# Two Mlps behind a delta-rule attention: three PSUM banks each for h and for the sums, an earlier third copy, and two steps moved from VectorE to GpSimd

## The chip, the core and the metric

The kernel runs on one core of a Trainium2 chip. The metric is the time of one execution in microseconds (us), here the median of three runs. A core has five engines with queues of their own, each strictly in order: TensorE (PE: matmuls, and PEld for the loads of their weights), VectorE (DVE), ScalarE (ACT), GpSimd (POOL) and SyncE (SP, which issues the DMAs). PE multiplies from SBUF into PSUM, which has eight banks of 128 partitions x 512 fp32 values. The engines wait for each other through semaphores.

## The reference

Three parts in a row, all in fp32; only the second is touched by the change, and it is the one shown in full.

```
attn: delta rule over 768 steps for 4 x 8 heads of 48 -> x [3072, 384]

def _moe_ref(x, w_in, w_out, a, b):          # first Mlp, d_ff = 2048
    h = x @ w_in
    P = a[0] + a[1]*h + a[2]*h**2 + a[3]*h**3
    Q = 1.0 + abs(b[0])*abs(h) + abs(b[1])*h**2
    g = P / (Q + 1e-6)
    return g @ w_out

def _moe2_ref(x, w_in, w_out):               # second Mlp
    h = x @ w_in
    return (h * tanh(softplus(h))) @ w_out
```

The weights come as 64-bit floats and are turned into two fp32 parts on the chip.

## The kernel before

**Splitting.** PE multiplies in a reduced fp32 format. So each operand is kept as a high part (a cast) and a low half (what the cast lost, a subtraction), and each product is three matmuls: high x high, high x low, low x high.

**Units.** The 3072 tokens are 6 groups of 512, and d_ff is 16 blocks of 128. A unit is one group and one block: 96 units per Mlp, numbered in the order of work, 16 to a group. For a unit PE forms h in one bank (9 matmuls, line 893) and, four units later, adds g times the second weights to three sums of the group (9 matmuls, line 1002). A sum takes a bank for 16 units. After the last unit of a group ACT copies the three sums out (line 1124, `ev`), and SP stores them.

**A unit of the first Mlp on the other engines.** ACT: magnitude of h (line 924, `q`), r = b1 q + b0 (line 931, or on POOL, line 927), s = a3 h + a2 (line 933). POOL: q = q r (line 937). ACT: Ln (line 945) and Exp with a minus sign (line 947), which give 1/Q. DVE: five steps for P and for g (lines 952, 954, 961, 965, 970); line 954 is the last to read h, so it frees h's bank. ACT casts g to its high part (line 904), POOL forms g's low half (line 908). r is on POOL in odd units, and also in the even unit of the three in which x is prepared.

**What sets the order.** Two strings, MLP_OPS, give the order in which the operations of one iteration are issued, and LAGS tells by how many units each lags behind: "u" is h, "d" the sums, "y" the copies, 1a 1b 1c magnitude, r and s, 1d q, 1e 1f Ln and Exp, 1g to 1k DVE's steps, 1L and 1m the parts of g. Each engine gets its own operations in that order and keeps to it. Within ACT, Ln and Exp of a unit stand ahead of the magnitude of the next.

**Around it.** "xa" and "xB" prepare the next group's x (line 873 casts on ACT, line 877 forms the low half); "fx" loads it. "c" and "f" convert the second Mlp's weights, half of them (16 sides) during the first: a side is a magnitude on ACT (line 739), clamp and shift on DVE (lines 744, 748), two more steps on DVE (754, 760), a cast on ACT (767) and a remainder on POOL (772, `wt`). `calm` lists the iterations in which a side goes on. In PSUM, `Ring` hands out 2 banks for h, 4 for sums and 2 for r in turn: `ps.add(ps2, h=2, o=4, r=2)`. With four banks for three sums, the first sum of a group starts in a bank that nobody holds.

Of the kernel before, what the change touches and what calls it, by code (L numbers as in the profile page):

```python
# [9 lines left out]
F32 = mybir.dt.float32  # L10
# [22 lines left out]


MLP_OPS = [
    "fx fw y0 y1 1e 1f u0 u1 u2 1a 1b 1c 1i 1j 1k 1d 1g 1h y2 d0 d1 d2 d3 xa 1L 1m xB f c",
    "fx fw y0 1e 1f y1 2a 2b u0 u1 u2 1i 1j 1k y2 d0 v0 2M d1 v1 d2 v2 d3 v3 xa 1L 1m xB f c",
]
LAGS = {
# [6 lines left out]
class Ring:  # L46
# [6 lines left out]
    def add(self, pool, **bufs):  # L53
        for tag, b in bufs.items():
            slots = self.slots.setdefault(tag, [])
            self.n[tag] = len(slots)
            slots.extend((pool, b) for _ in range(b))

    def tile(self, shape, dtype, tag):
        i = self.n[tag]  # L60
        self.n[tag] = (i + 1) % len(self.slots[tag])
        pool, b = self.slots[tag][i]
        return pool.tile(shape, dtype, tag=tag, name=tag, bufs=b)


# [628 lines left out]
class Weights:  # L694
# [5 lines left out]
    LEAST = 2.0 ** -15  # L700
    MOST = 1.875 * 2.0 ** 16
    free = False
    word = None

    def __init__(self, nc, w_in, w_out, sb, kept, passing, scratch):
# [14 lines left out]
    def convert(self, f, side):  # L720
        nc = self.nc
        w = {}

        def get():
            w["raw"] = self.sb.tile([128, 3, 128], I64, "w64")
            src = self.w_out[f * 128:(f + 1) * 128] if side else self.w_in[:, :, f * 128:(f + 1) * 128]
            nc.sync.dma_start(out=w["raw"], in_=src)

        def word(i):
            return w["raw"].rearrange("p k c -> p (k c)").bitcast(I32).rearrange("p (n t) -> p n t", t=2)[:, :, i]  # L730

        def mag():
            w["m"] = self.sb.tile([128, 384], I32, "wm")
            if self.free:
                nc.vector.tensor_scalar(
                    out=w["m"], in0=word(1), scalar1=0x7FFFFFFF, scalar2=None, op0=ALU.bitwise_and
                )
            else:
                nc.scalar.activation(out=w["m"].bitcast(F32), in_=word(1).bitcast(F32), func=ACTF.Abs)

        def size():
            m = w["m"]
            w["x"] = m if self.word is None else self.word.bitcast(I32)
            nc.vector.tensor_scalar(
                out=w["x"].bitcast(F32), in0=w["m"].bitcast(F32), scalar1=self.LEAST, scalar2=self.MOST,
                op0=ALU.max, op1=ALU.min,
            )
            nc.vector.tensor_scalar(
                out=w["x"], in0=w["x"], scalar1=3, scalar2=0x3FFFFFF8,
                op0=ALU.logical_shift_left, op1=ALU.bitwise_and,  # L750
            )

        def sign():
            nc.vector.scalar_tensor_tensor(
                out=w["x"], in0=word(1), scalar=-(1 << 30), in1=w["x"],
                op0=ALU.bitwise_and, op1=ALU.bitwise_or,
            )

        def low():
            nc.vector.scalar_tensor_tensor(  # L760
                out=w["m"], in0=word(0), scalar=29, in1=w["x"],
                op0=ALU.logical_shift_right, op1=ALU.bitwise_or,
            )

        def out():
            m = w["m"].bitcast(F32).rearrange("p (k c) -> p k c", k=3)
            nc.scalar.copy(out=self.tile(f)[:, 0, side], in_=m)

        def rest():
            t = self.tile(f)  # L770
            m = w["m"].bitcast(F32).rearrange("p (k c) -> p k c", k=3)
            nc.gpsimd.tensor_tensor(out=t[:, 1, side], in0=m, in1=t[:, 0, side].bitcast(F32), op=ALU.subtract)

        def done():
            if side and f in self.tag:
                self.store(f)

        return get, mag, size, sign, low, out, rest, done
# [267 lines left out]
def tile_delta_attention_two_mlps(  # L1046
# [59 lines left out]
    def starts(i):  # L1106
        return i == 0 or i == n1 or units[i][0] != units[i - 1][0]
# [70 lines left out]
    with ExitStack() as bctx:  # L1178
        sb2 = bctx.enter_context(tc.tile_pool(name="sb2", bufs=1, reuse_waits="tile"))
        ps2 = bctx.enter_context(tc.tile_pool(name="ps2", bufs=1, space=PSUM, reuse_waits="tile"))  # L1180
        sb.add(sb2, w=NF - FQ - FG, wt=1, w64=1, wm=1, x=1, q=3, s=3, r=2, g=3, gh=5 - FIRST, ev=3)
        ps.add(ps2, h=2, o=4, r=2)
        own = FQ + FG
        fetch_w = {n: (w1.fetch_split, own + LOOK + n) for n in range(NF - own - LOOK)}
        for f in range(DIRECT):
            fetch_w[n1 - NF + 6 + f] = (w2.fetch_split, f)
        calm = [i for i in range(CONV_START, n1 - 8) if not any(starts(i + 5 - k) for k in range(3))]
        for f in range(LOOK):
            w1.fetch_split(own + f)
        steps = [  # L1190
            (m1, "1a", m1.e1, [0]), (m1, "1b", m1.e1, [1]), (m1, "1c", m1.e1, [2]), (m1, "1d", m1.e2, None),
            (m1, "1e", m1.e3, [0]), (m1, "1f", m1.e3, [1]), (m1, "1g", m1.e4, [0]), (m1, "1h", m1.e4, [1]),
            (m1, "1i", m1.e5, [0]), (m1, "1j", m1.e5, [1]), (m1, "1k", m1.e5, [2]),
            (m1, "1l", m1.hi, "V"), (m1, "1L", m1.hi, "A"), (m1, "1P", m1.hi, "P"),
            (m1, "1m", m1.lo, "P"), (m1, "1M", m1.lo, "V"),
            (m2, "2a", m2.e1, None), (m2, "2b", m2.e2, None), (m2, "2M", m2.lo, None),
        ]
        steps = {name: (m, f, a) for m, name, f, a in steps}
        ups, downs = {}, {}
        m1.pool = {i for i in range(n1) if i % 2 or any(starts(j) for j in range(i + 3, i + 6) if j < n2)}  # L1200
        m2.pool = range(n1, n1 + NF)
        for i in range(n2 + max(LG.values())):
            kind = int(i >= n1)
            if i == CONV_START - 3:
                conv.start()

            def at_x(f):
                for k in range(3):
                    j = i + 5 - k
                    if 0 < j < n2 and starts(j):  # L1210
                        f(mlp(j))(units[j][0], k)

            for op in LISTS[kind]:
                if op in steps:
                    m, f, a = steps[op]
                    j = i - LG[op[0] + {"L": "l", "P": "l", "M": "m"}.get(op[1], op[1])]
                    if FIRST <= j < n2 and mlp(j) is m:
                        f(j, *([a] if a else []))
                elif op[0] == "u" and FIRST <= i < n2:
                    if i not in ups:  # L1220
                        ups[i] = mlp(i).up(i, *units[i])
                    n = int(op[1])
                    run(ups[i][3 * n:3 * n + 3])
                elif op[0] == "d" and 0 <= i - FIRST < FIRST:
                    if i - FIRST not in downs:
                        downs[i - FIRST] = down(i - FIRST)
                    n = int(op[1])
                    run(downs[i - FIRST][0][3 * n:3 * n + 3])
                elif op[0] in "dvy" and FIRST <= i - LAG - (op[0] == "y") < n2:
                    j = i - LAG - (op[0] == "y")  # L1230
                    if j not in downs:
                        downs[j] = down(j)
                    n = int(op[1])
                    if op[0] == "d":
                        run(downs[j][0][3 * n:3 * n + 3])
                    elif (op[0] == "y") == (j < n1):
                        run(downs[j][1][n:n + 1])
                elif op == "fw" and i in fetch_w:
                    fetch, f = fetch_w[i]
                    fetch(f)  # L1240
                elif op == "fx" and i + 8 < n2 and starts(i + 8):
                    mlp(i + 8).fetch_x(units[i + 8][0])
                elif op == "xa":
                    at_x(lambda m: m.x_hi)
                elif op == "xB":
                    at_x(lambda m: lambda g, k: m.x_lo(g, k, "V"))
                elif op == "c" and i > n1:
                    w2.free = True
                    w2.word = w2.word or ps.tile([128, TOK], F32, "r")[:, 0:384]
                    conv.pull(CONV_RATE)  # L1250
                elif op == "c" and i in calm:
                    conv.pull(6 * DIRECT * (calm.index(i) + 1) // len(calm) - conv.n)
                elif op == "f":
                    conv.flush()
# [29 lines left out]
```

## Time and profile before

| | us |
|---|---|
| median of 3 runs | 1126.9 (1125.48 to 1130.12) |
| the profiled execution, its time | 1126.43 |
| its span, first to last instruction | 1124.7 |
| PE busy | 1060.0 (94%) |
| DVE busy | 720.8 (64%) |
| ACT busy | 610.8 (54%) |
| POOL busy | 541.2 (48%) |

The shares are averages over three stages. The attention takes the first 320 us, the first Mlp lasts to about 725 us, the second to the end. PE's matmuls overlap, so a busy PE still may be stalling for some tenths of a us; and an engine that is busy all the time need not be the one that others wait for. The groups of rows further down are from the trace of this one execution; times in them count from the span's start.

### The profile page before, as it was taken

The page shows a single profiled execution, that of the slowest core. Times are in us where ns is not written, and L with a number is a line of the kernel's source. Part 1 is how long each engine was busy: PE and PEld are TensorE (multiplying, and loading weights), DVE is VectorE, ACT ScalarE, POOL GpSimd, SP SyncE. Part 2 cuts the span into 40 slices and gives each one's busy share as a digit, 9 for nine tenths or more (in the row PEclk, how much of TensorE's full clock was granted, in tenths as well). Part 3 has the DMA queues.
Part 4 walks back from the last instruction along what each step waited for, and adds up shares of the span by engine and source line. Part 5 has one row for each costly group of instructions (what it writes and reads, how often), then busy time and mean ns, then how long its engine had stood idle before and what let it go on. Part 6 is the DMA issues. An engine that isn't in the chain of part 4 may idle for free.

```text
span 1124.7 us, 24637 instructions
## 1 busy us (share of the span) xinstructions
PE 1060.0 (94%) x10172; PEld 920.8 (82%) x10172; DVE 720.8 (64%) x1207; ACT 610.8 (54%) x1100; POOL 541.2 (48%) x623
## 2 busy tenths in 40 slices
PE   6778988798989999999999999999999999999998
PEld 5668877688868778878887887899999999999997
DVE  5996577995669999999999999992121211212110
ACT  4524455233568888988889888743333223233322
POOL 4287778667447777777777877763000000000000
PEclk8996899995899999999999999999999999999999
DMA  7616877234473021121202036250101001010000
GB/s 146 140 29 163 201 206 199 46 88 101 102 267 141 15 99 43 57 71 62 94 15 98 15 141 239 67 172 1 57 1 57 1 11 46 1 57 1 29 1 28
DMA packets 120111, 92.91 MB, mean 83 GB/s; under 512 B 79680, under 2 KB 104384, under 8 KB 120000
## 3 DMA queue, kind: packets, MB, share of 16 engines
q1 hardware_dynamic: 119744, 91.25, 27.7%
q8 instruction: 79, 1.29, 0.5%
q14 instruction: 32, 0.26, 0.1%
q0 software_dynamic: 256, 0.10, 0.1%
HBM read 63.02 MB, written 28.31 MB: 81 GB/s over the span
## 4 chain that ended last, share of the span: by engine, by line
PE 50%; POOL 15%; DVE 12%; ACT 12%; issue 7%; DMA 3%; SPq 2%; POOLq 0%; DVEq 0%; ACTq 0%
PE h L893 20%; PE o L1035 18%; POOL q L937 7%; POOL gh L908 3%; PE o L1002 3%; ACT r L945 3%; POOL r L927 3%; PE c_ps L597 2%; ACT q L924 2%; ACT r L947 2%; PE y_ps L635 2%; DVE tmp L520 1%; SPq L310 1%; PE c_ps L580 1%; PE s_all L620 1%
## 5 line engine op out<-in xcount | busy, mean ns | idle before, releaser
L893 PE MATMUL h<-x,w 128*128 128x512 f32 x1278 | 318.0, 393 | 3.9 <-DVE s L954 3.6
L893 PEld LDWEIGHTS h<-x,w 128*128 128x128 f32 x1278 | 237.0, 188 | 56.5 <-DVE s L954 10.2
L908 DVE TENSOR_TENSOR gh<-g,gh 128x512 fp32r<-128x512 f32 x80 | 55.3, 692 | 282.8 <-ACT g L1026 282.8
L1021 ACT ACTIVATE gh<-h 128x512 fp32r<-128x512 f32 x96 | 57.5, 599 | 231.4 <-PE h L893 231.4
L1035 PE MATMUL o<-w,gh 128*128 128x384 f32 x864 | 162.5, 337 | 0.0
L1002 PE MATMUL o<-gh,w 128*128 128x512 f32 x648 | 159.2, 390 | 0.0
L1035 PEld LDWEIGHTS o<-w,gh 128*128 128x128 f32 x864 | 153.4, 188 | 6.0
L908 POOL TENSOR_TENSOR gh<-g,gh 128x512 fp32r<-128x512 f32 x110 | 142.6, 1297 | 23.8 <-ACT g L1026 21.4
L937 POOL TENSOR_TENSOR q<-q,r 128x512 f32<-128x512 f32 x94 | 122.0, 1297 | 61.6 <-ACT r L931 57.2
L1002 PEld LDWEIGHTS o<-gh,w 128*128 128x128 f32 x648 | 121.5, 188 | 26.0 <-ACT ev L1124 0.8
L893 PE MATMUL h<-x,wg 128*128 128x512 f32 x432 | 107.0, 392 | 2.8 <-DVE wm L760 1.6
L893 PEld LDWEIGHTS h<-x,wg 128*128 128x128 f32 x432 | 80.5, 188 | 19.9 <-DVE s L954 2.5
L945 ACT ACTIVATE r<-q,cst 128x512 f32<-128x512 f32 x94 | 65.0, 692 | 48.8 <-POOL q L937 48.7
L933 ACT ACTIVATE s<-h,ab 128x512 f32<-128x512 f32 x94 | 72.7, 774 | 0.0
L954 DVE SCALAR_TENSOR_TENSOR s<-s,ab,h 128x512 f32<-128x512 f32 x94 | 70.2, 747 | 3.3
L961 DVE SCALAR_TENSOR_TENSOR q<-q,r 128x512 f32<-128x512 f32 x94 | 63.8, 679 | 13.4 <-ACT r L947 13.1
L965 DVE SCALAR_TENSOR_TENSOR r<-s,ab,r 128x512 f32<-128x512 f32 x94 | 70.1, 745 | 0.0
L526 POOL TENSOR_TENSOR xs<-xs,tmp 128x30 f32<-128x30 f32 (+14 forms) x120 | 63.1, 526 | 9.4
L952 DVE TENSOR_TENSOR s<-s,h 128x512 f32<-128x512 f32 x94 | 63.8, 679 | 4.6 <-ACT s L933 4.6
L970 DVE SCALAR_TENSOR_TENSOR g<-q,r 128x512 f32<-128x512 f32 x94 | 64.5, 687 | 3.2
L520 POOL TENSOR_TENSOR tmp<-xs 128x30 f32<-128x30 f32 (+14 forms) x120 | 59.2, 493 | 7.4
L904 ACT CAST gh<-g 128x512 fp32r<-128x512 f32 x94 | 58.5, 623 | 0.0
(157 smaller groups left out, 1696.7 us busy)
## 6 DMA issues: line engine op xcount, KB each, us to landing
w<-w SPq DMA_DIRECT2D x24, 768.0 KB, 7.0
w<-in_moe_w_in_dram SPq DMA_DIRECT2D x32, 384.0 KB, 3.6
w<-in_moe_w_out_dram SPq DMA_DIRECT2D x32, 384.0 KB, 3.3
xraw<-x SPq DMA_DIRECT2D x36, 256.0 KB, 4.1
w<-wt SPq DMA_DIRECT2D x8, 768.0 KB, 3.4
kn<-in_k_dram SPq DMA_DIRECT2D x48, 96.0 KB, 3.6
gh<-in_q_dram SPq DMA_DIRECT2D x48, 96.0 KB, 3.3
v<-in_v_dram SPq DMA_DIRECT2D x48, 96.0 KB, 3.9
```

The lines of the kernel that those rows point to most:

```text
L520: eng.tensor_tensor(out=tv, in0=ls[:, j, j + 1:HC].unsqueeze(1).to_broadcast([128, j, n]), in1=xs[:, 0:j, j:j + 1].to_broadcast([128, j, n ...
L893: self.nc.tensor.matmul(out=self.st[i]["h"], lhsT=self.w.t[f][:, a, 0, k], rhs=self.x[g][:, b, k], start=(n == 0), stop=(n == 8),)
L908: (nc.gpsimd if engine == "P" else nc.vector).tensor_tensor(out=s["gh"][:, 1], in0=s["g"], in1=s["gh"][:, 0].bitcast(F32), op=ALU.subtract)
L933: nc.scalar.activation(out=s["s"], in_=s["h"], func=ACTF.Identity, scale=k["a3"], bias=k["a2"])
L937: nc.gpsimd.tensor_tensor(out=s["q"], in0=s["q"], in1=s["r"], op=ALU.mult)
L945: nc.scalar.activation(out=s["r"], in_=s["q"], func=ACTF.Ln, bias=k["c"])
L952: nc.vector.tensor_tensor(out=s["s"], in0=s["s"], in1=s["h"], op=ALU.mult)
L954: nc.vector.scalar_tensor_tensor(out=s["s"], in0=s["s"], scalar=k["a1"], in1=s["h"], op0=ALU.add, op1=ALU.mult)
L965: nc.vector.scalar_tensor_tensor(out=s["r"], in0=s["s"], scalar=k["a0"], in1=s["r"], op0=ALU.add, op1=ALU.mult)
L970: nc.vector.scalar_tensor_tensor(out=s["g"], in0=s["q"], scalar=2.0, in1=s["r"], op0=ALU.subtract, op1=ALU.mult, reverse0=True)
L1002: self.nc.tensor.matmul(out=self.acc[g][d], lhsT=self.w.t[f][:, a, 1, d], rhs=self.st[i]["gh"][:, b], start=(first and n == 0), stop=(last ...
L1035: self.nc.tensor.matmul(out=self.acc[g][t][:, 0:384], lhsT=self.st[i]["gh"][:, a, t * 128:(t + 1) * 128], rhs=self.w.t[f][:, b, 1].rearran ...
```

## The change

- PSUM in the first Mlp: three banks for h (two, and one lent, named `ho`) and three for the sums. When the second Mlp begins, `ho` goes back to the sums, which then have four, and h has two.
- The third copy of a group's sums, "y2", is issued behind Ln and Exp and ahead of the next magnitude; before it came behind s of that next unit.
- Weights: while `w2.ahead` holds (the first Mlp), POOL clamps the magnitude in place right behind ACT's magnitude. DVE keeps the shift and what follows.
- x of the first Mlp: POOL forms the low halves (before DVE). The three pieces are prepared 7, 5 and 3 iterations ahead of the group, in odd units, instead of 5, 4 and 3; x is loaded 12 iterations ahead instead of 8.
- r is on POOL in odd units alone. `calm` now leaves out the two iterations at the end of a group, not the three in which x is prepared.

```diff
-    "fx fw y0 y1 1e 1f u0 u1 u2 1a 1b 1c 1i 1j 1k 1d 1g 1h y2 d0 d1 d2 d3 xa 1L 1m xB f c",
+    "fx fw y0 y1 1e 1f y2 u0 u1 u2 1a 1b 1c 1i 1j 1k 1d 1g 1h d0 d1 d2 d3 xa 1L 1m xB f c",
...
+    def lend(self, pool, tag, to, back=None):
+        if back:
+            self.slots[back].pop()
+            self.n[back] %= len(self.slots[back])
+        self.n[to] = len(self.slots[to])
+        self.slots[to].append((pool, 1, tag))
...
+            if self.ahead:
+                clamp(nc.gpsimd, w["m"])
+
+        def clamp(engine, out):
+            engine.tensor_scalar(
+                out=out.bitcast(F32), in0=w["m"].bitcast(F32), scalar1=self.LEAST, scalar2=self.MOST,
+                op0=ALU.max, op1=ALU.min,
+            )
...
-        ps.add(ps2, h=2, o=4, r=2)
+        ps.add(ps2, h=2, o=3, r=2)
+        ps.lend(ps2, "ho", "h")
...
-        calm = [i for i in range(CONV_START, n1 - 8) if not any(starts(i + 5 - k) for k in range(3))]
+        calm = [i for i in range(CONV_START, n1 - 8) if not any(starts(i - 4 - k) for k in range(2))]
...
-        m1.pool = {i for i in range(n1) if i % 2 or any(starts(j) for j in range(i + 3, i + 6) if j < n2)}
+        m1.pool = range(1, n1, 2)
...
                 for k in range(3):
+                    j = i + 7 - 2 * k
+                    if 0 < j < n1 and starts(j):
+                        f(m1)(units[j][0], k)
                     j = i + 5 - k
-                    if 0 < j < n2 and starts(j):
-                        f(mlp(j))(units[j][0], k)
-
+                    if n1 <= j < n2 and starts(j):
+                        f(m2)(units[j][0], k)
+
+            if i == n1:
+                ps.lend(ps2, "ho", "o", "h")
...
-                    at_x(lambda m: lambda g, k: m.x_lo(g, k, "V"))
+                    at_x(lambda m: lambda g, k: m.x_lo(g, k, "P" if m is m1 else "V"))
```

The queue of ACT at the end of the first group, before: from the two first copies, over Ln and Exp of unit 19, to unit 20. `q<-h` is the magnitude, `ev<-o` a copy of a sum.

```order
L1124 COPY ev<-o 128x512 x2
L945 ACTIVATE r<-q,cst 128x512
L947 ACTIVATE r<-r 128x512
L924 ACTIVATE q<-h 128x512
L931 ACTIVATE r<-q,ab 128x512
L933 ACTIVATE s<-h,ab 128x512
L1124 COPY ev<-o 128x512
L904 CAST gh<-g 128x512
```

The same place in the changed kernel, whose lines are numbered some 13 higher:

```order
L1137 COPY ev<-o 128x512 x2
L958 ACTIVATE r<-q,cst 128x512
L960 ACTIVATE r<-r 128x512
L1137 COPY ev<-o 128x512
L937 ACTIVATE q<-ho 128x512
L944 ACTIVATE r<-q,ab 128x512
L946 ACTIVATE s<-ho,ab 128x512
L917 CAST gh<-g 128x512
```

The third copy has moved from behind unit 20's s to ahead of its magnitude.

The queue of POOL in units 57 to 60, before; `q<-q,r` opens a unit, `gh` is g's low half, `wt` a weight's remainder, and `r<-q,ab` is r of the next unit.

```order
L937 TENSOR_TENSOR q<-q,r 128x512
L908 TENSOR_TENSOR gh<-g,gh 128x512
L772 TENSOR_TENSOR wt<-wm,wt 128x384
L937 TENSOR_TENSOR q<-q,r 128x512
L908 TENSOR_TENSOR gh<-g,gh 128x512
L927 TENSOR_SCALAR r<-q,ab 128x512
L937 TENSOR_TENSOR q<-q,r 128x512
L908 TENSOR_TENSOR gh<-g,gh 128x512
L927 TENSOR_SCALAR r<-q,ab 128x512
L937 TENSOR_TENSOR q<-q,r 128x512
```

And in the changed kernel; `x<-xraw,x` is a low half of x, `wm<-wm` the clamp:

```order
L950 TENSOR_TENSOR q<-q,r 128x512
L921 TENSOR_TENSOR gh<-g,gh 128x512
L890 TENSOR_TENSOR x<-xraw,x 128x512
L785 TENSOR_TENSOR wt<-wm,wt 128x384
L950 TENSOR_TENSOR q<-q,r 128x512
L921 TENSOR_TENSOR gh<-g,gh 128x512
L940 TENSOR_SCALAR r<-q,ab 128x512
L950 TENSOR_TENSOR q<-q,r 128x512
L921 TENSOR_TENSOR gh<-g,gh 128x512
L890 TENSOR_TENSOR x<-xraw,x 128x512
L752 TENSOR_SCALAR wm<-wm 128x384
L950 TENSOR_TENSOR q<-q,r 128x512
```

A low half of x now stands between g's low half in unit 57, and in 59, and q of the next unit, with a remainder or a clamp behind it; r of unit 60 has gone from the queue, as ACT has it now.

## Rows read from the trace of the kernel before

**Rows 1.** Stretches: PE, PEld, DVE, ACT, POOL busy us (count), clock, DMA share, GB/s.

```profile
252.00:280.00 28.00, 24.67 (x612) 23.02 (x613) 14.64 (x29) 9.21 (x20) 21.96 (x37) 0.60 0.44 109
308.00:336.00 28.00, 23.05 (x353) 19.35 (x353) 18.89 (x32) 17.38 (x30) 13.06 (x12) 1.00 0.70 248
345.00:701.00 356.00, 352.71 (x1535) 285.89 (x1534) 340.36 (x507) 309.81 (x527) 272.10 (x236) 1.00 0.22 78
```

**Rows 2.** Waits, 345 to 725 us: waiter <- releaser: total us, times, longest.

```profile
POOL q L937 <- ACT r L931: 50.6, 38, 1.6
ACT r L945 <- POOL q L937: 44.7, 68, 1.3
...
PEld h L893 <- DVE s L954: 10.5, 21, 1.0
```

**Rows 3.** Groups by line, ACT, 345 to 725 us: busy, mean ns | idle before.

```profile
L924 ACT ACTIVATE q<-h 128x512 f32<-128x512 f32 x88 | 52.3, 595 | 0.0
```

**Rows 4.** Timeline, ACT, magnitudes of units 46 to 48: start, us taken, instruction.

```profile
506.00 0.59 ACT L924 ACTIVATE q<-h 128x512 f32<-128x512 f32 x1
...
510.07 0.59 ACT L924 ACTIVATE q<-h 128x512 f32<-128x512 f32 x1
...
514.24 0.59 ACT L924 ACTIVATE q<-h 128x512 f32<-128x512 f32 x1
```

**Rows 5.** Timeline, POOL, units 46 and 47; in brackets the idle time before.

```profile
507.52 1.30 POOL L937 TENSOR_TENSOR q<-q,r 128x512 f32<-128x512 f32 x1 [1.52 <-ACT r L931]
508.78 1.29 POOL L908 TENSOR_TENSOR gh<-g,gh 128x512 fp32r<-128x512 f32 x1
510.84 0.77 POOL L927 TENSOR_SCALAR r<-q,ab 128x512 f32<-128x512 f32 x1 [0.77 <-ACT q L924]
511.69 1.29 POOL L937 TENSOR_TENSOR q<-q,r 128x512 f32<-128x512 f32 x1
512.95 1.29 POOL L908 TENSOR_TENSOR gh<-g,gh 128x512 fp32r<-128x512 f32 x1
```

**Rows 6.** Timeline, ACT, the magnitudes of units 2 and 94, 92 units apart.

```profile
321.75 0.60 ACT L924 ACTIVATE q<-h 128x512 f32<-128x512 f32 x1 [1.90 <-PE h L893]
...
705.75 0.60 ACT L924 ACTIVATE q<-h 128x512 f32<-128x512 f32 x1
```

**Rows 7.** Timeline, PE, two sums a unit apart; h of units 85 and 95.

```profile
428.63 2.20 PE L1002 MATMUL o<-gh,w 128*128 128x512 f32 x9
...
432.71 2.20 PE L1002 MATMUL o<-gh,w 128*128 128x512 f32 x9
...
663.66 2.20 PE L893 MATMUL h<-x,wg 128*128 128x512 f32 x9
...
705.74 2.23 PE L893 MATMUL h<-x,w 128*128 128x512 f32 x9
```

**Rows 8.** Timeline, ACT, units 20 and 21 at a group's end; unit 83's magnitude.

```profile
397.03 0.59 ACT L924 ACTIVATE q<-h 128x512 f32<-128x512 f32 x1
...
399.05 0.57 ACT L1124 COPY ev<-o 128x512 f32<-128x512 f32 x1
399.51 0.62 ACT L904 CAST gh<-g 128x512 fp32r<-128x512 f32 x1
...
401.25 0.59 ACT L924 ACTIVATE q<-h 128x512 f32<-128x512 f32 x1
...
659.50 0.59 ACT L924 ACTIVATE q<-h 128x512 f32<-128x512 f32 x1
```

**Rows 9.** Timeline, POOL, remainders of weights in units 11 and 18.

```profile
362.96 1.47 POOL L772 TENSOR_TENSOR wt<-wm,wt 128x384 fp32r<-128x384 f32 x1
...
392.41 1.13 POOL L772 TENSOR_TENSOR wt<-wm,wt 128x384 fp32r<-128x384 f32 x1
```

**Rows 10.** Groups by line, POOL, 280 to 292 us.

```profile
L877 POOL TENSOR_TENSOR x<-xraw,x 128x512 fp32r<-128x512 f32 x3 | 3.8, 1270 | 0.0
L772 POOL TENSOR_TENSOR wg<-wm,wg 128x384 fp32r<-128x384 f32 x2 | 2.0, 1002 | 6.9 <-ACT wg L767 6.9
```

More of the change, by code (lines that the diff above doesn't have):

```diff
@@ L56, in add @@
             self.n[tag] = len(slots)
-            slots.extend((pool, b) for _ in range(b))
+            slots.extend((pool, b, tag) for _ in range(b))
+    def lend(self, pool, tag, to, back=None):
[4 more added lines that the diff above has]
+        self.slots[to].append((pool, 1, tag))
     def tile(self, shape, dtype, tag):
@@ L61, in tile @@
         self.n[tag] = (i + 1) % len(self.slots[tag])
-        pool, b = self.slots[tag][i]
+        pool, b, tag = self.slots[tag][i]
         return pool.tile(shape, dtype, tag=tag, name=tag, bufs=b)
@@ L702 @@
     free = False
+    ahead = False
     word = None
@@ L739, in mag, with size @@
                 nc.scalar.activation(out=w["m"].bitcast(F32), in_=word(1).bitcast(F32), func=ACTF.Abs)
[L741 to L745, printed above, removed]
+            if self.ahead:
[3 more added lines that the diff above has]
+                out=out.bitcast(F32), in0=w["m"].bitcast(F32), scalar1=self.LEAST, scalar2=self.MOST,
                 op0=ALU.max, op1=ALU.min,
             )
+        def size():
+            w["x"] = w["m"] if self.word is None else self.word.bitcast(I32)
+            if not self.ahead:
+                clamp(nc.vector, w["x"])
             nc.vector.tensor_scalar(
-                out=w["x"], in0=w["x"], scalar1=3, scalar2=0x3FFFFFF8,
+                out=w["x"], in0=w["m"] if self.ahead else w["x"], scalar1=3, scalar2=0x3FFFFFF8,
                 op0=ALU.logical_shift_left, op1=ALU.bitwise_and,
@@ L1205, in tile_delta_attention_two_mlps @@
                 conv.start()
+                w2.ahead = True
             def at_x(f):
                 for k in range(3):
+                    j = i + 7 - 2 * k
+                    if 0 < j < n1 and starts(j):
+                        f(m1)(units[j][0], k)
                     j = i + 5 - k
-                    if 0 < j < n2 and starts(j):
-                        f(mlp(j))(units[j][0], k)
+                    if n1 <= j < n2 and starts(j):
+                        f(m2)(units[j][0], k)
+            if i == n1:
+                ps.lend(ps2, "ho", "o", "h")
             for op in LISTS[kind]:
@@ L1240, in tile_delta_attention_two_mlps @@
                     fetch(f)
-                elif op == "fx" and i + 8 < n2 and starts(i + 8):
-                    mlp(i + 8).fetch_x(units[i + 8][0])
+                elif op == "fx":
+                    for j in ((i + 12,) if i + 12 < n1 else ()) + ((i + 8,) if n1 <= i + 8 < n2 else ()):
+                        if starts(j):
+                            mlp(j).fetch_x(units[j][0])
                 elif op == "xa":
@@ L1245, in tile_delta_attention_two_mlps @@
                 elif op == "xB":
-                    at_x(lambda m: lambda g, k: m.x_lo(g, k, "V"))
+                    at_x(lambda m: lambda g, k: m.x_lo(g, k, "P" if m is m1 else "V"))
                 elif op == "c" and i > n1:
-                    w2.free = True
+                    w2.free, w2.ahead = True, False
                     w2.word = w2.word or ps.tile([128, TOK], F32, "r")[:, 0:384]
```

## The prediction, made before the changed kernel was run

> **What bounds the kernel now.** I read the busy time by stretch first, then the table of waits, then the timelines of ScalarE (ACT) and GpSimd (POOL). The change touches only the first Mlp (about 320 to 725 us). There TensorE (PE) looks like the bound: between 345 and 701 us it is busy 352.71 of 356 us at clock 1.00, and VectorE (DVE) 340.36 [rows 1]. That would make both look worth relieving. The table of waits says otherwise. ACT waits for POOL's product q 68 times (44.7 us), POOL waits for ACT's r 38 times (50.6 us), and PE waits 21 times (10.5 us) for the DVE step that frees a bank of h [rows 2]. Two engines that wait for each other in turn are a loop. The line to look at is ACT's first step of a unit, the magnitude of h: its idle time ahead of it, over 88 of them, is 0.0 us [rows 3]. So h was always there already: no unit starts when PE has delivered, it starts when ACT has finished the Exp of the unit before.
>
> The loop of a unit runs: magnitude (ACT), r (ACT in even units, POOL in odd ones), q (POOL), Ln and Exp (ACT), next magnitude. Two quiet units take 510.07 - 506.00 = 4.07 us (even) and 514.24 - 510.07 = 4.17 us (odd) [rows 4], 4.12 on average. PE's nine and nine matmuls need 432.71 - 428.63 = 4.08 us [rows 7]. The loop is slower than PE even undisturbed, and really took (705.75 - 321.75) / 92 = 4.174 us a unit [rows 6]. PE therefore runs ahead until both banks of h are full and then waits. These waits are the symptom: 92 x (4.174 - 4.08) = 8.6 us is what PE loses over the stage.
>
> **The change part by part.** The sum is made against the profiled execution's own 1126.43 us (span 1124.7), 0.5 us below the median of 1126.9.
>
> *Three banks for h.* PE may run one unit further ahead. Since ACT never waits for h, this speeds nothing in the loop: 0 us. It would count only if PE carried the lead into the second Mlp; the last item says why it can't.
>
> *Three banks for the sums and the earlier third copy.* The four banks let a new group's first sum start in a free bank; now each of its three sums needs the matching copy. ACT's third copy moves from inside the next even unit to between Exp and the next magnitude, that is into the loop. A copy holds ACT's queue for 399.51 - 399.05 = 0.46 us; where it stood it lengthened its unit from 4.07 to 401.25 - 397.03 = 4.22 us, by 0.15 [rows 4, 8]. So 5 ends of a group x (0.46 - 0.15) = **+1.6 us**. (The sixth end lies in the second Mlp's order and doesn't change.)
>
> *Low halves of x on POOL.* Fifteen instructions of 1.27 us [rows 10] leave DVE. DVE is not in the loop, so that gives nothing. On POOL they come in odd units behind the low half of g. POOL's next instruction follows a tensor_tensor after 508.78 - 507.52 = 1.26 us, so POOL is free at 512.95 + 1.26 = 514.21, and is wanted again for the even unit's q at 514.24 + (507.52 - 506.00) = 515.76 [rows 4, 5]: room for 1.55 us. One low half fits, with 0.28 to spare. But the order puts a weight remainder behind it in units 11, 57, 73 and 77. That takes 1.00 to 1.13 us [rows 9, 10], so q is 0.72 to 0.85 late: 4 x 0.78 = **+3.1 us**. One such delay goes: in unit 11 of before, the remainder took 1.47 us [rows 9] and, against the pattern (r starts 510.84 - 508.78 = 2.06 after the low half of g [rows 5]), held r up by 1.26 + 1.47 - 2.06 = 0.67: **-0.65 us**.
>
> *Clamps on POOL.* The trace has no clamp on POOL. The nearest row is POOL's tensor_scalar r, 0.77 us for 512 elements [rows 5]; for 384 I estimate 0.58. The slow bound is POOL's 384-element tensor_tensor, 1.00 [rows 10]; the fast bound is no cost at all, which would take only the 0.6 below away. Alone behind an odd unit it has the 1.55 us of room, behind an even one 510.84 - (508.78 + 1.26) = 0.80: free at 0.58; at 1.00 it would cost 8 x 0.20 = 1.6. Behind a low half of x (units 43 and 59) it is 0.58 - 0.28 = 0.30 late: **+0.6 us** (1.4 at 1.00). DVE's 16 clamps again give nothing, as DVE is not waited for in the loop.
>
> *Small ones.* Weight remainders behind even units remain eight; each may run at 1.00 or at 1.13 us, +-1.0 us in all. r of one even unit per group returns to ACT, conversion work shifts by an iteration: together **-0.1 us**. The earlier loads of x (SyncE's queue) land units before they are used, 0.
>
> *Where PE ends.* The last end of a group sets PE back to the loop. In unit 83 the third copy now starts where the next magnitude would have, at 659.50 + 4.17, and ends 0.57 later [rows 4, 8]; then three matmuls (3 x 4.08 / 18 = 0.68) and the next unit's h starts at about 659.50 + 5.5 instead of 663.66 = 659.50 + 4.16 [rows 7, 8]. From there PE does ten units undisturbed, 40.8 us, and is at 659.50 + 46.3; before it lost time on banks and was at 705.74 = 659.50 + 46.24 [rows 7]. So **+0.1 us**: the waits on h turn into waits for the copies.
>
> Sum: 1.6 + 3.1 - 0.65 + 0.6 - 0.1 + 0.1 = +4.65, so 1126.43 + 4.65 = **1131 us**. With the clamp at 1.00 (+2.4), the remainders' +-1.0 and low halves slowed as the remainder in [rows 9] was (0.2 each behind the four, +0.8), this case's own range is 1129 to 1134.
>
> The remainder shown at 1.13 us ran beside DVE's clamp and shift; the one of 1.00 did not [rows 9, 10]. The Trainium skill (SBUF — State Buffer, Who interferes with whom) says that DVE and GpSimd share one pair of ports, held for a whole instruction by a DVE tensor_scalar in a two-port mode or a DVE instruction with two inputs in SBUF, so that the other blocks. By it, taking clamps and low halves off DVE quickens POOL: the sum would be 1 us lower, at 1130; by the row alone it stays at 1131.
>
> **The rivals.**
>
> *The clock falls.* At the first end of a group PE comes with its whole new lead. Before, PE ended unit 95's h at 705.74 + 2.04 and its magnitude began at 705.75 + 4.07: a lead of 2.0 us [rows 6, 7]. The third bank adds at most one unit, 4.08. I estimate from these that PE idles 2 to 3 us ahead of the first copy and 1 us ahead of the third, in one place. The clock stood at 1.00 in 308 to 336 us with PE busy 23.05 of 28, and at 0.60 in 252 to 280 with 24.67 busy in short matmuls [rows 1], so busy time alone doesn't tell. If a unit then runs at 1.2 GHz, PE loses up to 4.08 us, of which its remaining lead hides 1 to 2: about 1133. The Trainium skill (TensorE: Matmul & The Clock Gate, HAM oscillation) says that PE waiting between bursts brings the half clock back; no row of this stage shows it.
>
> *PE was the bound after all.* Then the third bank takes the 8.6 us away, and five ends give back about 0.7 each: 1126.4 - 8.6 + 3.5 = 1121, faster. For it: PE's 99% busy. Against: the 0.0 in [rows 3].
>
> *POOL's additions fit.* If the remainder comes late enough or the queue has slack that the quiet pair doesn't show, 3.1 + 0.6 fall away: 1127.5, no change. Against: POOL is in order and its waits in the loop are for ACT, not spare time.
>
> **How the numbers follow.** The forecast has 0.60, the clock 0.16, the fitting POOL 0.14, PE as the bound 0.10. What a measurement can tell from no change is 0.5%, 5.6 us: beyond 1132.5 or below 1121.3. Slower: a third of the forecast's case (0.18) and most of the clock's (0.14), 0.32. Faster: half of PE's case and a little, 0.06. Same: 0.62. The range 1125.5 to 1134.5 leaves out most of PE's case, the slow end of the clock's and the edges of the forecast.
>
> **What would show it.** Right: in the changed kernel the magnitude of h still shows no idle time for PE; magnitude to magnitude is about 4.6 us in units 19, 35, 51, 67, 83 and about 4.8 to 4.9 in units 12, 58, 74, 78; PE no longer waits for DVE but for ACT's copies, most at the first end; DVE has idle time; POOL's idle time before q shrinks. Wrong: the magnitude waits for PE, or the 92 units take under 384 us; a half clock within 320 to 725 us is the first rival.

## The result, and the profile after

| | before | changed |
|---|---|---|
| median of 6 runs, us | 1126.97 | 1139.07 |
| lowest to highest, us | 1120.18 to 1130.12 | 1131.07 to 1146.86 |
| profiled execution: time / span, us | 1126.43 / 1124.7 | 1139.03 / 1137.3 |
| unit 2's to unit 94's magnitude (92 units), us | 384.0 | 396.8 |

The changed kernel is slower: its time is 1.0117 of before, 95% interval 1.0067 to 1.0166. The forecast was 1131 with a range to 1134.5, so the direction was right and the size was not.

The 92 units took 396.77 us, 12.77 more than in [rows 6]; the span grew by 12.6. So the first Mlp accounts for it. ACT's timeline of the changed kernel, the two ends of the 92 units:

```profile
321.01 0.60 ACT L937 ACTIVATE q<-ho 128x512 f32<-128x512 f32 x1 [1.88 <-PE ho L906]
...
717.78 0.59 ACT L937 ACTIVATE q<-h 128x512 f32<-128x512 f32 x1
```

The loop still decides. The groups by line of the changed kernel, ACT, 345 to 738 us (`ho` is the lent bank), answer to [rows 3]: over 88 magnitudes ACT waited for h for 0.2 us, once.

```profile
L937 ACT ACTIVATE q<-h 128x512 f32<-128x512 f32 x58 | 34.5, 595 | 0.2 <-PE h L906 0.2
L937 ACT ACTIVATE q<-ho 128x512 f32<-128x512 f32 x30 | 17.9, 595 | 0.0
```

The waits of the same stretch (total us, times, longest) answer to [rows 2]. PE's waits for DVE are gone from the table, and PE waits for ACT's copies instead; POOL's wait for r has shrunk from 50.6 to 31.3, because POOL now has other work to do there, while ACT's wait for POOL has grown from 44.7 to 51.5.

```profile
ACT r L958 <- POOL q L950: 51.5, 71, 2.1
DVE q L974 <- ACT r L960: 32.5, 39, 2.0
POOL q L950 <- ACT r L944: 31.3, 25, 2.0
...
PEld o L1015 <- ACT ev L1137: 18.9, 10, 3.3
PE o L1015 <- ACT ev L1137: 14.3, 8, 2.9
```

In stretches (columns as in [rows 1]) DVE is no longer full: 327.36 of 369 us. That bought nothing.

```profile
345.00:714.00 369.00, 353.06 (x1520) 286.46 (x1520) 327.36 (x476) 315.92 (x535) 313.42 (x261) 0.99 0.21 74
```

POOL's groups by line, 330 to 738 us, hold the surprise. The clamp (L752) takes 1584 ns for 384 elements, twice what r takes for 512.

```profile
L940 POOL TENSOR_SCALAR r<-q,ab 128x512 f32<-128x512 f32 x46 | 35.5, 771 | 22.8 <-ACT q L937 22.8
L752 POOL TENSOR_SCALAR wm<-wm 128x384 f32<-128x384 f32 x17 | 26.9, 1584 | 0.0
L890 POOL TENSOR_TENSOR x<-xraw,x 128x512 fp32r<-128x512 f32 x15 | 22.0, 1468 | 0.0
L785 POOL TENSOR_TENSOR wt<-wm,wt 128x384 fp32r<-128x384 f32 x16 | 16.9, 1053 | 0.0
```

What that does to a unit stands in POOL's timeline around unit 60: low half of x 1.61, clamp 1.49, and only then q, at 573.63. In a quiet even unit q starts 1.52 after the magnitude; unit 60's magnitude was at 570.64, so q was 1.47 late.

```profile
570.59 1.61 POOL L890 TENSOR_TENSOR x<-xraw,x 128x512 fp32r<-128x512 f32 x1
572.17 1.49 POOL L752 TENSOR_SCALAR wm<-wm 128x384 f32<-128x384 f32 x1
573.63 1.30 POOL L950 TENSOR_TENSOR q<-q,r 128x512 f32<-128x512 f32 x1
```

ACT's timeline shows the price: from unit 60's magnitude to unit 61's it is 5.55 us instead of 4.07.

```profile
570.64 0.59 ACT L937 ACTIVATE q<-h 128x512 f32<-128x512 f32 x1
...
576.19 0.59 ACT L937 ACTIVATE q<-h 128x512 f32<-128x512 f32 x1
```

### The profile page after: what moved, and what is told of

It reads as the page before. It is cut to its first block, busy times and chain, and to the rows that moved or that the text cites. A ratio compares the mean times of both kernels' runs of the same rounds, so it can differ in the third digit from the quotient of the medians.

```text
span 1137.3 us, 24635 instructions
## 1 busy us (share of the span) xinstructions
PE 1061.6 (93%) x10172; PEld 923.9 (81%) x10172; DVE 708.2 (62%) x1176; ACT 616.7 (54%) x1106; POOL 582.3 (51%) x649
## 3 DMA queue, kind: packets, MB, share of 16 engines
q8 instruction: 79, 1.29, 0.5%
## 4 chain that ended last, share of the span: by engine, by line
PE 57%; POOL 15%; DVE 10%; ACT 8%; issue 5%; DMA 3%; SPq 1%; POOLq 0%; DVEq 0%; ACTq 0%
PE h L906 21%; PE o L1048 13%; POOL q L950 7%; PE o L1015 6%; PE ho L1048 4%; POOL gh L921 4%; PE y_ps L642 3%; PE c_ps L604 2%; PE ho L906 2%; POOL r L940 2%; ACT r L958 2%; PE c_ps L587 2%; DVE tmp L527 1%; ACT q L937 1%; PE s_all L627 1%
## 5 line engine op out<-in xcount | busy, mean ns | idle before, releaser
L906 PE MATMUL h<-x,w 128*128 128x512 f32 x1062 | 262.8, 392 | 0.0
L906 PEld LDWEIGHTS h<-x,w 128*128 128x128 f32 x1062 | 198.3, 188 | 38.2
L1015 PE MATMUL o<-gh,w 128*128 128x512 f32 x648 | 165.5, 398 | 15.9 <-ACT ev L1137 14.3
L1048 PE MATMUL o<-w,gh 128*128 128x384 f32 x648 | 135.3, 337 | 0.0
L1048 PEld LDWEIGHTS o<-w,gh 128*128 128x128 f32 x648 | 116.1, 188 | 0.0
L906 PE MATMUL h<-x,wg 128*128 128x512 f32 x360 | 89.6, 393 | 0.0
L906 PEld LDWEIGHTS h<-x,wg 128*128 128x128 f32 x360 | 67.8, 189 | 13.5
L1048 PE MATMUL ho<-w,gh 128*128 128x384 f32 x216 | 58.8, 335 | 0.0
L785 POOL TENSOR_TENSOR w<-wm,w 128x384 fp32r<-128x384 f32 x40 | 41.8, 1047 | 32.8 <-ACT w L780 32.7
L1039 ACT ACTIVATE g<-h 128x512 f32<-128x512 f32 x96 | 57.2, 595 | 0.0
## 6 DMA issues: line engine op xcount, KB each, us to landing
w<-in_moe_w_in_dram SPq DMA_DIRECT2D x32, 384.0 KB, 3.7
w<-in_moe_w_out_dram SPq DMA_DIRECT2D x32, 384.0 KB, 3.2
```

The source lines that it names most:

```text
L906: self.nc.tensor.matmul(out=self.st[i]["h"], lhsT=self.w.t[f][:, a, 0, k], rhs=self.x[g][:, b, k], start=(n == 0), stop=(n == 8),)
L1015: self.nc.tensor.matmul(out=self.acc[g][d], lhsT=self.w.t[f][:, a, 1, d], rhs=self.st[i]["gh"][:, b], start=(first and n == 0), stop=(last ...
L1048: self.nc.tensor.matmul(out=self.acc[g][t][:, 0:384], lhsT=self.st[i]["gh"][:, a, t * 128:(t + 1) * 128], rhs=self.w.t[f][:, b, 1].rearran ...
```

## The experiments

The start of the stage moves by itself: over the profiles here unit 2's magnitude lies between 315.45 and 323.77 us although the attention's code is the same. So the kernels are compared by the 92 units, measured like [rows 6], and by their time, with an interval where a kernel was run more than once. Each kernel's 92 units are those of one profile.

| kernel | 92 units, us | time over before's, interval |
|---|---|---|
| before | 384.0 | |
| changed | 396.8 | 1.0117 (1.0067 to 1.0166) |
| changed, clamp on VectorE | 388.8 | 1.0038 (1.0007 to 1.0070) |
| before, clamp on GpSimd | 392.0 | one run, 1133.1 us |
| changed, four forms of clamp | 393.2 | one run, 1138.5 us |
| before, three and three banks, early copy | 385.7 | 1.0007 (0.9980 to 1.0035) |
| before, three and three banks, late copy | 397.1 | one run, 1140.6 us |
| odd units | 384.6 | 0.9997 (0.9974 to 1.0020) |
| odd units, banks and early copy | 386.4 | one run, 1122.5 us |
| odd units, late start | 381.6 | 0.9976 (0.9948 to 1.0004) |
| the same, third copy on VectorE | 381.1 | 0.9973 (0.9943 to 1.0003) |

**The clamp undone.** The edit on the changed kernel:

```diff
-                w2.ahead = True
+                w2.ahead = False
```

> The changed kernel with one part undone: the clamp of the magnitudes is on VectorE again, all else as changed. Theory (the clamp on GpSimd is what was mis-sized: 1.5 to 1.8 us each instead of the 0.58 estimated, and 17 of them stand in the loop's way): the 92 units from the magnitude of unit 2 to that of unit 94, 396.8 us in the changed kernel and 384.0 before, take 387.5 to 388.5 us; the time is about 8 to 9 us below the changed kernel's, near 1130.5; unit pairs 28/29, 48/49, 44 and 60 fall back from 5.0 to 5.5 us to 4.1 to 4.3; the remainders behind low halves of x in units 12, 58, 74, 78 still cost 0.65 to 0.8 each. Rival (GpSimd is slowed by the low halves of x and the remainders, whatever the clamp does): the 92 units stay above 393 us.

The 92 units took 388.84 us, 0.3 above the upper end expected: 7.93 of the 12.77 were the clamp's. Units 44 and 60 fell from 5.23 and 5.55 us to 4.07 and 4.08, unit 49 from 5.05 to 4.18, unit 29 only to 4.52. The remainders behind low halves of x stayed: units 12, 58, 74 and 78 took 4.97, 4.74, 4.97 and 4.73. The rival falls. Time fell to 1.0038 of before, 1131.93 us median.

**The clamp alone.** Before, with the part of the change that adds `clamp` and `ahead`, and nothing else.

> The kernel before with one part done alone: GpSimd clamps the magnitudes, nothing else changed. Theory: a clamp takes 1.5 to 1.8 us there too; behind an even unit's low half of g there is room for 0.80, so the seven in even units cost about 0.6 to 0.9 each, the two in units 43 and 59 (whose next unit has r on GpSimd) about 0.75 each, the others up to 0.2: the 92 units go from 384.0 to 389.5 to 391.5 us, the time to about 1133. Rival (the clamp is slow only because the other new work on GpSimd or VectorE's new order stands beside it): clamps of about 0.6 us and 92 units in 384 to 385 us.

392.03 us, 8.0 more than before and 0.5 above the upper end expected; units 44 and 60 took 1.18 us more each, where 0.75 was expected. So the clamp costs the same 8 us with or without the rest of the change. POOL's clamps, 330 to 730 us, were no faster without the low halves of x beside them:

```profile
L745 POOL TENSOR_SCALAR wm<-wm 128x384 f32<-128x384 f32 x17 | 28.7, 1688 | 0.0
```

**What makes the clamp slow.** Four forms in turn, the edit shortened (each comment gives what that form has in place of the clamp's constants and operations):

```diff
         def clamp(engine, out):
+            form = (2 * f + side) % 4 if engine is nc.gpsimd else 0
+            if form == 1:   # scalar1=lim[0], scalar2=lim[1], op0=ALU.max, op1=ALU.min
+            if form == 2:   # scalar1=1.0, scalar2=0.0, op0=ALU.mult, op1=ALU.add
+            if form == 3:   # scalar1=lim[2], scalar2=lim[3], op0=ALU.mult, op1=ALU.add
```

> The changed kernel with four forms of GpSimd's clamp in turn over the sides: max and min with constants in the instruction (as changed), max and min with constants from SBUF, times 1 plus 0 with constants in the instruction, times 1 plus 0 with constants from SBUF (the last is the form of GpSimd's r, 0.77 us for 512 elements; the last two forms do not clamp). Theory A (max and min are slow on GpSimd): the first two take 1.5 us, the last two about 0.6. Theory B (constants in the instruction are slow): first and third 1.5, second and fourth 0.6. Theory C (the place or the operand in SBUF is slow): all four 1.5. By A or B half of the clamps shrink and the 92 units take about 392 us instead of 396.8.

POOL's groups by line, 330 to 740 us. L771 is the form as changed, L754 max and min with constants from SBUF (`lim`), L760 times and plus with constants in the instruction, L766 times and plus with constants from SBUF:

```profile
L771 POOL TENSOR_SCALAR wm<-wm 128x384 f32<-128x384 f32 x5 | 7.5, 1492 | 0.4
L754 POOL TENSOR_SCALAR wm<-wm,lim 128x384 f32<-128x384 f32 x4 | 7.2, 1795 | 0.0
L766 POOL TENSOR_SCALAR wm<-wm,lim 128x384 f32<-128x384 f32 x4 | 3.6, 891 | 0.0
...
L760 POOL TENSOR_SCALAR wm<-wm 128x384 f32<-128x384 f32 x4 | 2.1, 513 | 0.4
```

Theory A holds: max and min take 1492 ns where times and plus take 513, on the same kind of tile, with the same kind of constants. The means of the two forms with constants from SBUF mislead, because most of their turns are those in which the changed kernel's clamp, too, takes 1.80 us instead of 1.49 (the point on the port pair below says beside what). Where nothing delays them they take 0.15 us more than with constants in the instruction, as POOL's timeline shows:

```profile
352.70 1.64 POOL L754 TENSOR_SCALAR wm<-wm,lim 128x384 f32<-128x384 f32 x1
...
573.20 0.66 POOL L766 TENSOR_SCALAR wm<-wm,lim 128x384 f32<-128x384 f32 x1
```

The 92 units fell to 393.19 us (about 392 expected). Which of max and min is the slow one, or whether it is both, was not tried.

**Banks and the early copy alone.** The edit on before:

```diff
-        ps.add(ps2, h=2, o=4, r=2)
+        ps.add(ps2, h=2, o=3, r=2)
+        ps.lend(ps2, "ho", "h")
...
+            if i == n1:
+                ps.lend(ps2, "ho", "o", "h")
```

and `y2` ahead of the magnitude, as in the change.

> The kernel before with one part done alone: three banks for h, three for the sums, third copy ahead of the next magnitude; clamps, x and the conversion's iterations as before. Theory (the loop of ScalarE and GpSimd is the bound): nothing is gained from the third bank; the third copy costs 0.46 instead of 0.15 us per end of a group, so the 92 units take 385.5 to 386 us instead of 384.0, TensorE's waits for VectorE's step on h go from 10 us to near 0 and come back as waits for ScalarE's copies at the five ends; time about 1128. Rival (TensorE's bank waits were a cost of their own): 92 units under 380 us and a time near 1121.

385.67 us, as the loop theory has it (+1.67), and a time that can't be told from before's. The waits of that kernel, 345 to 725 us, show PE's waits changing their name: in the row of its weight loads 10.5 us for DVE in [rows 2], now 11.4 us for ACT's copies.

```profile
PEld o L1009 <- ACT ev L1131: 11.4, 10, 3.3
...
PE o L1009 <- ACT ev L1131: 7.2, 8, 2.9
```

**Banks without the early copy.** The same without the `y2` edit.

> The kernel before with three banks for h and three for the sums, but the third copy left in its old place, inside the next even unit. Theory: the loop is as before, 384.0 us for the 92 units (0.15 us per end of a group, as before); but a new group's third sum then waits for a copy that ends about 2.6 us after the next magnitude, so at the last end TensorE starts unit 85's h about 7.6 us after unit 83's magnitude instead of 5.5, and the second Mlp's first sum comes about 408 to 409 us after unit 2's magnitude (406.45 before, 408.2 with the third copy sooner). So the earlier copy buys no time on balance, it only moves the wait. Rival (the later copy holds TensorE up at every end and the loop then waits for TensorE): the 92 units take over 386 us and the magnitude shows idle time for TensorE.

Here my theory failed and its rival held: 397.08 us, 11.4 more than with the early copy. PE's timeline and ACT's at the first end of a group (unit 20's magnitude is at 396.82):

```profile
399.45 0.96 PE L1009 MATMUL o<-gh,w 128*128 128x512 f32 x3 [2.67 <-ACT ev L1131]
400.25 3.56 PE L900 MATMUL h<-x,wg 128*128 128x512 f32 x9
```

```profile
398.83 0.57 ACT L1131 COPY ev<-o 128x512 f32<-128x512 f32 x1
...
403.85 0.60 ACT L931 ACTIVATE q<-h 128x512 f32<-128x512 f32 x1 [2.72 <-PE h L900]
```

One us of that h, with the clock (columns as in [rows 1]):

```profile
401.00:402.00 1.00, 1.00 (x4) 0.76 (x3) 1.00 (x2) 0.12 (x1) 0.28 (x1) 0.50 0.00 0
```

The third sum waits for the late copy, PE issues the next h only after it, and that h then takes 3.56 us instead of 2.20, because the clock has fallen to 1.2 GHz (0.50 in the last row). So ACT waits 2.72 us for h, about half of it for the copy and half for the clock: at the ends of a group PE does become the bound. I had followed the wait to PE's lead at the last end and not asked whether the loop would run dry at each one.

**Odd units.** From what the runs had shown so far: banks, copies and clamp as before, x as changed, and the conversion in odd units alone. The edit on the changed kernel's `calm`:

```diff
+        calm = {}
+        for i in range(4, n1 - 8):
+            part, u = len(calm) % 3, (i + 1) % 16
+            if len(calm) < 6 * DIRECT and (part == 1 or u % 2 and (part == 0 or u not in (9, 11, 13))):
+                calm[i] = part
...
+                    conv.pull(1)
```

> A version made from what the runs show: banks and third copy as before (two for h, four for the sums), clamp on VectorE as before, low halves of x on GpSimd in odd units as changed, and the conversion's magnitudes and remainders put in odd units alone, remainders never behind a low half of x, where GpSimd has 1.55 us of room. Theory (the loop decides, and what stands within that room is free): quiet pairs of 4.07 and 4.17 and five ends of a group give 379.0 + 5 x 0.15 + 4 x 0.14, 380 to 381 us for the 92 units instead of 384.0, and a time 3 to 4 us below before, near 1122.5. Rival (VectorE, busy 340 of 356 us before, is as much the bound): the 92 units stay at 383 to 385 us although GpSimd no longer delays q.

384.60 us, which by the number is the rival's. But unit 4 alone took 7.64 us: I had also let the conversion begin two units sooner, and its first magnitude waited for its DMA, as ACT's timeline shows.

```profile
336.92 0.55 ACT L747 ACTIVATE wm<-w 128x384 f32<-128x384 f32 x1 [3.36 <-DMA w<-in_moe_w_in_dram]
```

Without these 3.5 us it would be 381.1, 0.1 above the theory's 380 to 381. That is arithmetic, so it was run (below).

> The version above with three banks for h, three for the sums and the earlier third copy. Theory: the third bank still gives nothing and the copy costs 0.31 more at each of five ends: 92 units in 381.5 to 382.5 us. Rival (with a quicker loop TensorE is near its own pace, and the third bank lets it take up what is left): 92 units in 379 us or less.

386.41 us, outside both ranges because unit 4 waits for its DMA here too (7.63 us), and 1.8 more than without the banks and the earlier copy (expected +1.5): the third bank gives nothing to a quicker loop either.

**Odd units, started where before starts.** `range(CONV_START, n1 - 8)`, and the first remainder allowed in unit 10.

> The odd-unit version with the conversion's start back where it was (its first magnitude had waited 3.36 us for its DMA in unit 4, and the stage took 384.6 us with that, about 381.1 without). Theory: no unit waits for a DMA, and the 92 units take 381 to 382 us against 384.0 before; the time is 2 to 3.5 us below before, near 1123. Rival (the 3.4 us come back as waits elsewhere, VectorE's or TensorE's): 383.5 us or more for the 92 units.

381.59 us, 2.4 below before; unit 4, with no DMA to wait for, took 4.05 us, and POOL's additions lie in the room as meant (but for the one allowed in unit 10: unit 11 took 4.52). In POOL's timeline the remainder in an odd unit ends at 443.47 and q starts, still after an idle 0.55, when ACT has r:

```profile
442.45 1.02 POOL L785 TENSOR_TENSOR wt<-wm,wt 128x384 fp32r<-128x384 f32 x1
444.02 1.31 POOL L950 TENSOR_TENSOR q<-q,r 128x512 f32<-128x512 f32 x1 [0.55 <-ACT r L944]
```

> The same with the third copy of a group's sums on VectorE. Theory: it leaves ScalarE's queue, so 0.15 us per end of a group goes: 92 units in 380 to 381 us, 0.5 to 1 us below the version above, which the time can hardly show. Rival (VectorE, with 0.6 us more at each end, is late for what ScalarE needs): 92 units longer than in the version above.

381.08 us, 0.5 less, as expected; the copy is `nc.vector.tensor_copy` where d is 2. Both have medians some 3 us below before's in the same runs (1121.26 and 1121.81 against 1124.83), but the intervals of their times reach 1.0004 and 1.0003. They beat the changed kernel; that they beat before is seen in the 92 units of one profile each and not settled by the time.

## Why the prediction was wrong, point by point

- **What bounds the kernel: right.** ACT never waited for h in before and for 0.2 us in the changed kernel; relieving PE's banks and DVE gained nothing.
- **The third bank and the early copy: right.** +1.6 us forecast, +1.67 measured with that part alone; in the changed kernel the five units at the ends of a group took 4.62 to 4.84 us, forecast 4.6.
- **Low halves of x and remainders: right in kind, 0.8 us low in sum.** Changed kernel without the clamp against banks and copy alone: 388.84 - 385.67 = 3.2 us. Forecast: 3.1 for the collisions less 0.75 for what goes, that is 2.35. Each late remainder cost 0.67 to 0.80 in the changed kernel, forecast 0.72 to 0.85; the rest lies in small shifts of other units, within the +-1.0 that the prediction allowed for them.
- **The clamp: this is the step that failed.** I took it from POOL's tensor_scalar r, times and plus, at 0.58 us, and gave +0.6. It takes 1.5 to 1.8 us, and cost 7.9 us (8.0 by itself). Even the slow bound, 1.00 us and 3.0 in all (2.4 above the 0.6), lay below. Scaling r's time to fewer elements was nearly right: r's own form took 0.66 us on the clamp's tile where nothing delayed it. The operations were what the row could not stand for. The rule by which the time then costs was right: with 1.58 in place of 0.58 it gives 8 x (1.58 - 0.80) + 2 x (1.58 - 0.28) = 8.8 us, and the clamp cost eight odd units 0.53 to 0.87 us each and units 44 and 60 1.16 and 1.47 (changed kernel against clamp on VectorE). Behind an even unit's low half of g there is 0.80 us, and r of the next unit came up to 0.9 late; behind a low half of x in unit 59 the whole 1.47 fell on q. POOL's timeline in units 28 and 29 shows the first case, r pushed from 436.48 (0.77 behind the magnitude at 435.71) to 437.36:

```profile
435.57 1.80 POOL L752 TENSOR_SCALAR wm<-wm 128x384 f32<-128x384 f32 x1
437.36 0.77 POOL L940 TENSOR_SCALAR r<-q,ab 128x512 f32<-128x512 f32 x1
```

- **Where PE ends: right where the clock held.** From unit 94's magnitude to the second Mlp's first sum it was 22.45 us before and 22.53 with banks and early copy alone: +0.1, as forecast. In the changed kernel it was 23.46, +1.0; the next point has the difference.
- **The clock: it fell, and cost about 1 us.** PE's timeline at the first end of a group shows 2.62 us idle, waiting for the first copy (forecast 2 to 3); then nine matmuls take 3.64 us instead of 2.20. The stretch around it has a mean clock of 0.79, and within it the clock stands at 0.50, which is 1.2 GHz. The same happened at the third and fifth ends. At the second and fourth PE was idle for 2.05 and 1.96 us, and the clock stayed at 1.00.

```profile
395.82 3.64 PE L1015 MATMUL o<-gh,w 128*128 128x512 f32 x9 [2.62 <-ACT ev L1137]
```

```profile
394.00:402.00 8.00, 6.18 (x21) 4.94 (x22) 7.37 (x11) 7.72 (x15) 5.60 (x5) 0.79 0.26 92
397.00:398.00 1.00, 1.00 (x4) 0.81 (x3) 1.00 (x3) 0.97 (x3) 0.64 (x1) 0.50 0.00 0
```

Within the 92 units PE's lead covered all but the 0.2 us that ACT waited for h. Behind the fifth end there was none to cover it: PE's next h there took 2.75 us.

```profile
677.45 2.75 PE L906 MATMUL h<-x,wg 128*128 128x512 f32 x9
```

With four forms of clamp the clock stayed at 1.00 at that end, the same h took 2.21 us, and the way from unit 94's magnitude to the second Mlp was 22.58 us instead of 23.46 (with the clamp on VectorE, where the clock fell at that end too, 23.15). So the rival's event came, at about half of its 2 us, and it wasn't the cause of the miss, though the prediction's last sign names it as the first rival to look at. The Trainium skill (TensorE: Matmul & The Clock Gate, HAM oscillation) has idle PE between bursts bring back the half clock; here the trace agrees at three of the five ends. In the kernel with the late copy the same fall was part of a real cost, since PE had no lead there.
- **The port pair: overlaps that fit it show, and they go with 1.8 us instead of 1.5.** Five of the 17 clamps took 1.80 or 1.81 us and the others 1.48 to 1.50. Each of the five began while VectorE's L767, which reads w and wm from SBUF, was under way, and none of the twelve did. DVE's timeline shows it for the clamp of 435.57 above:

```profile
435.10 0.93 DVE L767 SCALAR_TENSOR_TENSOR wm<-w,wm 128x384 int32<-128x384 int32 x1
```

In the kernel with the clamp alone ten of 17 took 1.79 to 1.93, each beside that step or a low half of x on VectorE. A VectorE step with h or r, which lie in PSUM, as its second input delayed no clamp. The remainders went from 1.10 to 1.05 us on average, 16 of them, under 1 us in all, much as the prediction had it. But what moved to POOL met the steps that stayed on VectorE: five times 0.31 us for the clamps, at most 1.6 of the 7.9, and the prediction had no term for that. The overlaps fit the rule on the ports that the prediction cites; no run tells the ports from another cause.
- **PE as the bound, POOL's additions fitting: both fell**, the first by the banks alone, the second by units 12, 58, 74 and 78.

With the clamp at its measured cost in place of 0.6, the sum would have been 4.65 - 0.6 + 7.9 = 12.0 us, 1138.4, against 1139.03 in the profiled execution. That it comes so close is in part luck: the low halves of x with the remainders, and PE's way to the second Mlp, took 0.8 and 0.9 us more than forecast, while the stage began 0.74 us earlier and what follows its end took 0.44 less, for which the prediction had no term. Its own range didn't follow from its terms either: 1131 with 2.4, 1.0 and 0.8 added is 1135, not 1134.

## What to carry to other kernels

A unit that never waits for the busiest engine isn't bound by it: look at the idle time ahead of the first instruction of the loop, and follow the loop through the engines that wait for each other. Work moved to an engine inside that loop is free only up to the room behind each of its instructions, so its duration must be known for that very operation; if no row has it, measure it by itself or bound it by far more than the next form. And a bank taken from one ring is paid for in the other: the early copy made three banks bearable, and in no run here did the third bank gain anything.

## What the runs showed of the hardware that was not expected

On GpSimd a tensor_scalar with max and min took 1.49 us on 128x384 fp32, with times and plus 0.51 us, constants in the instruction; constants from SBUF added 0.15 us to either. On VectorE the clamp had taken 0.66 us on average in the kernel before. Beside a VectorE step that reads two tiles from SBUF (L767) the clamp on GpSimd took 1.80 us.

The same low half of x took 1.27 us on GpSimd in the quiet end of the attention. In the first Mlp it took 1.29 or 1.30 us five times, 1.42 three times beside VectorE's shift (L761), and 1.61 or 1.62 seven times beside VectorE's L767 or L773, 1.47 on average.
